# Block-sparse attention with an ELU feed-forward layer on one core: how K reaches the score matmuls, and who makes the chunk bounds

## The chip, the cores and the metric

The kernel runs on one core of a Trainium2 chip. The metric is the device time of one execution in microseconds (us). Three timed runs of the kernel before took 306.54, 306.47 and 304.36 us, median 306.47 us. The profile is one further execution of 304.14 us, whose instructions span 302.4 us.

## The reference

`q`, `k` and `v` are float32 of shape (4, 8, 768, 64): 4 batches, 8 heads, 768 positions, 64 features. Keys are cut into 24 chunks of 32 positions. For each query an upper bound on its scores in each chunk is made from the chunk's minimum and maximum key, the 6 best causal chunks are kept, and ordinary softmax attention runs over the kept keys. Two matrix products with ELU between them follow.

```python
k_chunks = k.reshape(B, H, nc, chunk, D)
k_min, k_max = np.min(k_chunks, axis=3), np.max(k_chunks, axis=3)
ub = np.sum(np.maximum(q[:, :, :, None, :] * k_min[:, :, None, :, :],
                       q[:, :, :, None, :] * k_max[:, :, None, :, :]), axis=-1)
ub = np.where(causal, ub, -1e9)
top_chunks = np.argsort(ub, axis=-1)[..., -6:]
scores = scale * np.matmul(q, k.transpose(0, 1, 3, 2))
scores = np.where(sel & causal_within, scores, -1e9)
x = softmax(scores) @ v                     # then (B*S, H*D) = (3072, 512)
h = x @ w_in                                # (3072, 2048)
g = np.where(h > 0.0, h, np.exp(np.minimum(h, 0.0)) - 1.0)
out = g @ w_out                             # (3072, 512)
```

## The kernel before

**Blocks and pairs.** The 3072 rows are nine query blocks (`BLOCKS`): batch 0 gives blocks 0 to 2 of 256 rows, batches 1 to 3 give blocks 3 to 8 of 384 rows, two each. Heads go in pairs, j = 0 to 3, so that a pair's 2 x 64 features fill 128 partitions. A tile is 128 positions.

**Front of a block** (`front`, lines 746 to 752). K, Q and V tiles are loaded as float32, 128 positions by 8 heads by 64 features, 256 KB each (`load`, L439). `prep_k` turns a pair's K tiles by TensorE into PSUM (`turn_in`, L480). VectorE reduces the turned K twice, maximum and minimum over each chunk of 32 columns (L500), and subtracts (L517); the results are the `ksts` operands of the bounds. ScalarE then copies the turned K to bfloat16: for blocks 0 and 1 straight into `lhs` (L507), for the others into a buffer `kb` (L512), from which SyncE's queue issues two transfers a pair into `lhs` (L515). `prep_q` does the same turning for Q (L480, L530, L538, L541). `select` multiplies the bounds on TensorE (L559), finds the sixth best chunk on VectorE (L570, L577, L581) and writes 0/1 rows into partitions 64 to 95 of `rhs`, either by VectorE (L587, blocks 0 to 2) or by VectorE and a transfer (L593, L597).

**Mask rows.** `lhs` has 96 used partitions: 64 features of K and 32 rows with -40000 in row c at the columns of chunk c. A score matmul over 96 rows (`scores`, L621) thus gives the score, plus -40000 where the chunk was not selected. The mask rows are made once (`make_eone`, `make_econst`, `init_lhs`): VectorE fills four of the eight `lhs` tensors (L415), four transfers fill the others (L417).

**Attention and feed-forward.** `attend`: scores (L621), exponent on ScalarE (L637, L641), the diagonal's triangle on VectorE (L648, L655), product with V (L670), division (L679, L681), turning to `xt` by a transposing transfer on SyncE's queue (L694) or by TensorE (L689). `mlp`: L709 on TensorE, exponent on ScalarE (L713), minus one on GpSimd (L715), `max`/`min` on VectorE to `gT` (L717), L728 on TensorE, copy out on ScalarE (L732), store (L735). V is cast to bfloat16 by GpSimd (`cast_v`, L471).

**Order.** Every operation is first only listed, with an assumed cost, a priority and its dependences. `Plan.run` then plays the list through, engine by engine, with limited buffers (`CAPS`) and a table of shifts of the priorities by stage and engine (`SHIFTS`); the order that comes out is the order in which the instructions are written to each engine, and each engine works through its own in that order. Loads named in `SW_LOADS` and the weights are issued by GpSimd in the order of `SW_ORDER`, after a small copy that waits for the first K load (L782). TensorE gets filler matmuls on a zero tile where the plan leaves it idle in its first 70 us (L836).

Of the kernel before, what the change touches and what calls it, by code (L numbers as in the profile page):

```python
# [48 lines left out]
DIRECT_K = (0,1)  # L49
# [4 lines left out]
SW_LOADS = ("v0", "q1", "v1", "k2", "q2", "v2")  # L54
ACT_LOADS = ("k0", "q0", "k1")
SW_ORDER = ("v0", "q1", "v1", "wi0", "wi1", "wi2", "wi3", "k2", "q2", "v2", "wo0", "wo1", "wo2", "wo3")
QC_ACT = (0, 1)
VC_ACT = ()
# [5 lines left out]
CAPS = dict(psT=1, psS=2, psO=1, psM=4, kld=2, qld=2, vld=1, QTf=6, Qrl=6, kb=3, kmx=3, ubT=2, thr=2,  # L64
            msk=2, pt=9, rcp=2, on=3, xt=12, gT=6, e=4, osb=2)
RING = 64
FILL_NS = 500
# [3 lines left out]
    ('cast', 'POOL'): (20.57252, 6.8612, 30.20405, 34.41781, 25.32335, 14.40461, 26.6349, 11.90162, 25.68724),  # L71
    ('gate', 'POOL'): (13.59135, 0.0, 0.0, 0.0, 0.0, 0.0, 0.0, 0.0, 0.0),
    ('init', 'POOL'): (0.0, 2.28733, 0.0, 0.0, 0.0, 0.0, 0.0, 0.0, 0.0),
    ('init', 'SP'): (0.0, 0.0, -9.16794, 0.0, 0.0, 0.0, 0.0, 0.0, 0.0),
    ('kld', 'ACT'): (8.44149, -3.35541, 0.0, 0.0, 0.0, 0.0, 0.0, 0.0, 0.0),
    ('kld', 'SP'): (2.64524, 1.41433, 0.0, 19.17193, 19.24991, 15.09263, 15.30211, 16.29283, 21.31107),
    ('kld', 'POOL'): (0.0, 0.0, 0.38774, 0.0, 0.0, 0.0, 0.0, 0.0, 0.0),
    ('mlp_in', 'ACT'): (-0.05814, -2.04884, 12.26157, -1.88135, -2.65088, -4.49011, 9.3327, 8.76113, -19.73093),
    ('mlp_in', 'DVE'): (-1.73242, 3.97867, -1.47336, 9.41966, -10.49042, -8.87396, -12.71275, -12.8411, -15.53763),
    ('mlp_in', 'PE'): (4.09513, -2.56825, 21.51914, 0.57236, -12.4212, 2.60542, -2.43752, -8.17452, 3.48831),  # L80
    ('mlp_in', 'POOL'): (-2.43649, 11.70673, 2.23367, -14.23721, -5.69178, 14.90153, -11.32679, 8.9361, -11.19179),
    ('mlp_out', 'ACT'): (-12.88274, 0.81443, 16.77095, 16.67571, -11.88345, 9.70583, 0.95732, -8.4172, -1.17404),
    ('mlp_out', 'PE'): (13.70296, 13.79101, 25.0585, 31.67234, 12.47262, 15.64879, 21.01371, 0.27209, 18.2925),
    ('mlp_out', 'SP'): (-3.30971, -11.51233, -15.89764, -18.24659, -18.60542, -17.81261, -26.35693, -42.75655, -13.10907),
    ('prep_k', 'ACT'): (25.42091, 28.44317, 23.77021, 23.42552, 13.97171, 21.34953, 15.42692, 18.62561, 8.78796),
    ('prep_k', 'DVE'): (-0.54594, 19.16199, -1.31495, -4.02643, 4.07559, 21.34444, 2.30963, 13.60589, 3.98678),
    ('prep_k', 'PE'): (-11.58195, 3.17776, 12.63442, -8.97337, 3.48395, 2.91992, -14.39538, 4.89175, 2.89372),
    ('prep_k', 'SP'): (0.0, 0.0, -5.13913, -2.5227, -2.19514, 2.12301, -17.34079, 2.83345, -3.2583),
    ('prep_q', 'ACT'): (-5.44132, 13.02836, -8.90449, 17.58325, 14.42173, 12.5627, 34.41294, 25.56545, -14.46432),
    ('prep_q', 'DVE'): (34.05268, 22.68609, 13.28254, 24.29798, 22.86233, 18.30023, 26.52607, 17.39426, -1.03575),  # L90
    ('prep_q', 'PE'): (1.55827, 3.21992, -10.06088, -5.14194, -2.06832, 11.30076, 4.84068, 13.28142, -17.29924),
    ('prep_q', 'POOL'): (0.0, 0.0, 5.34856, 19.77789, 11.98652, -3.89053, 10.37057, 11.76628, -23.71212),
    ('qld', 'ACT'): (3.03879, 0.0, 0.0, 0.0, 0.0, 0.0, 0.0, 0.0, 0.0),
    ('qld', 'SP'): (-1.86639, 0.0, 0.0, 4.4756, 10.84559, 7.56364, -2.78613, 8.55013, 3.96718),
    ('qld', 'POOL'): (0.0, -13.20166, -16.00657, 0.0, 0.0, 0.0, 0.0, 0.0, 0.0),
    ('score', 'ACT'): (10.38182, 13.98097, 9.11548, 19.0005, 2.98314, 27.9414, -1.05566, 1.31311, 14.18917),
    ('score', 'DVE'): (-19.79772, 4.15071, 2.99001, -22.45535, -14.99666, -19.5343, -10.56439, -19.58759, -3.51749),
    ('score', 'PE'): (-4.26638, 7.52896, -6.42214, -0.75335, 6.37057, 12.51955, 6.09242, -2.75776, -4.26028),
    ('select', 'DVE'): (0.47921, -15.73633, 7.03029, -0.12414, -12.38193, 6.31401, -10.30796, 14.19953, -5.33831),
    ('select', 'PE'): (-24.6966, -18.87682, -19.68284, -16.23997, -30.84817, 2.75471, -0.87585, -4.04933, -12.62166),  # L100
    ('select', 'SP'): (0.0, 0.0, 0.0, -13.44596, -16.7602, -5.46409, -14.4042, 14.89348, -7.20168),
    ('vld', 'POOL'): (8.78219, 3.38089, -2.61859, 0.0, 0.0, 0.0, 0.0, 0.0, 0.0),
    ('vld', 'SP'): (0.0, 0.0, 0.0, 33.2739, 30.57728, 28.35083, 33.49035, 19.69352, 14.95572),
    ('w_in', 'POOL'): (-4.9889, 0.0, 0.0, 0.0, 0.0, 0.0, 0.0, 0.0, 0.0),
    ('w_out', 'POOL'): (-8.71011, 0.0, 0.0, 0.0, 0.0, 0.0, 0.0, 0.0, 0.0),
    ('weigh', 'DVE'): (11.1506, -8.59523, 21.73165, 3.04344, -9.17916, -0.955, 14.23334, -3.50298, 13.22401),
    ('weigh', 'PE'): (-14.42242, 4.04006, -5.56916, -12.49286, -15.03128, -12.17144, 11.16201, -20.81204, -2.27982),
    ('weigh', 'SP'): (0.0, -24.05575, -20.27905, -10.4246, -14.45262, -3.75467, -21.17209, -15.72941, 0.0),
# [41 lines left out]
class Plan:  # L150
# [37 lines left out]
    def run(self):  # L188
# [41 lines left out]
        while True:  # L230
# [37 lines left out]
            if done is not None:  # L268
                done.end = clock + 750
                lanes[done.eng][done.lane] = done.end  # L270
                dirty.update(("SP", "ACT", "POOL"))
                leave(done, done.end)
                enter(done, done.end, True)
                continue
# [23 lines left out]
            else:  # L298
                o.end = t + o.occ + o.lat
# [7 lines left out]
def kernel(  # L307
# [37 lines left out]
    econst = fix([P, NCH, CHUNK], BF16, "econst")  # L345
    eone = fix([P, NCH], BF16, "eone")
# [3 lines left out]
    vexts = [fix([P, NQT, 2, D + 1], BF16, f"vext{s}") for s in range(NSET)]  # L350
    lhs = [fix([P, 2, S], BF16, f"lhs{s}") for s in range(NSET)]
    ksts = [fix([P, 2, NPAIR, CHUNK], F32, f"kst{x}") for x in range(2)]
    rhs = [fix([P, 2, NPAIR, w], BF16, f"rhs{x}") for x, w in enumerate((QMAX, QMAX, 256))]
# [4 lines left out]
    r_ident_f, r_ident_b, r_tri, r_econst, r_eone = res(), res(), res(), res(), res()  # L358
# [3 lines left out]
    r_lhs = [[res() for _ in range(3)] for _ in range(NSET)]  # L362
# [4 lines left out]
    RH = [{(0, 256): 0, (256, 512): 1, (512, 768): 2, (0, 384): 0, (384, 768): 1}[lo, hi] for (_b, _x, lo, hi) in BLOCKS]  # L367
# [25 lines left out]
    def make_eone():  # L393
        nc.gpsimd.memset(eone[64:96], MASKNEG)
        nc.gpsimd.affine_select(out=eone[64:96], in_=eone[64:96], compare_op=AOT.is_equal, fill=0.0, base=0,
                                pattern=[[1, NCH]], channel_multiplier=-1)

    pool_op(200, make_eone, [r_eone])
    pool_op(540, make_ident_f, [r_ident_f])

# [27 lines left out]
    def load(dst, x, i, cls, at):  # L428
# [5 lines left out]
        for n in range(nt):  # L434
# [9 lines left out]
            if e == "SP":  # L444
                chain[:] = [o]
# [422 lines left out]
```

## Time and profile before

| what | before |
|---|---|
| timed runs, median (lowest to highest) | 306.47 us (304.36 to 306.54) |
| the profiled execution, and its span | 304.14 us, 302.4 us |
| TensorE matmul busy | 279.0 us, 92% |
| VectorE, ScalarE, GpSimd busy | 204.9, 201.3, 138.9 us |
| mean granted TensorE clock | 0.960 |
| turning K on TensorE (L480) | 88 + 8 matmuls of 128 columns |
| VectorE reductions of K (L500) | 48 of 384 columns, 16 of 256 columns |
| ScalarE copies of K (L507, L512) | 16 and 28 |
| transfers from `kb` to `lhs` (L515) | 56, all issued by SyncE |

The page gives for each engine the time in which an instruction ran; matmuls overlap in the pipeline, so a busy TensorE is not one at its peak. The chain of waits follows the last instruction back to what released it. In a table by windows, the first column is the stretch of time, then its length, then busy time by engine with the number of instructions in parentheses, the granted clock, the mean busy share of the DMA engines, and GB/s. In a timeline, the columns are start, length, engine, line and operation; neighbouring instructions of one kind are merged with their number.

### The profile page before, as it was taken

What the parts mean: (1) busy time and instruction counts of PE and PEld (TensorE: products, weight loads), DVE (VectorE), ACT (ScalarE), POOL (GpSimd) and SP (SyncE); (2) the same over time, 40 slices, a digit from 0 to 9 for tenths busy, and PEclk for the clock granted to TensorE, in tenths of its full rate; (3) what the DMA queues carried; (4) which work ended last, traced back from release to release, by engine and by line L of the source; (5) the groups of instructions that cost most, each with busy time, mean ns of one, the idle gap of its engine ahead of it and who ended that gap; (6) DMA issues with size and microseconds to landing.
All of it is one profiled execution on the core that took longest, in us unless ns stands there. A gap on an engine that the chain in (4) does not pass through costs nothing.

```text
span 302.4 us, 7251 instructions
## 1 busy us (share of the span) xinstructions
PE 279.0 (92%) x2521; PEld 177.4 (59%) x2521; DVE 204.9 (68%) x658; ACT 201.3 (67%) x458; POOL 138.9 (46%) x285
## 2 busy tenths in 40 slices
PE   7466878999999899999999989999999999999994
PEld 7235645677857645666665546666556666554541
DVE  4567488799666979768579955874866646680420
ACT  1764767579829725997797259886398896671521
POOL 8796674024817624571069322581535100570420
PEclk9955797999999999999999999999999999999999
DMA  8769996149292565658239853924111012100101
GB/s 194 204 130 196 292 220 115 41 125 244 48 222 74 133 149 135 162 153 204 81 80 219 191 166 84 233 57 128 47 44 43 3 48 63 30 21 37 67 37 70
DMA packets 88805, 36.23 MB, mean 120 GB/s; under 512 B 76224, under 2 KB 84928, under 8 KB 88768
## 3 DMA queue, kind: packets, MB, share of 16 engines
q1 hardware_dynamic: 80464, 27.64, 36.3%
q0 software_dynamic: 5184, 7.34, 12.0%
q10 hardware_dynamic: 3120, 0.79, 1.2%
q8 instruction: 20, 0.33, 0.4%
q14 instruction: 17, 0.14, 0.1%
HBM read 27.26 MB, written 6.29 MB: 111 GB/s over the span
## 4 chain that ended last, share of the span: by engine, by line
PE 64%; DVE 14%; DMA 7%; POOL 6%; SPq 3%; ACT 2%; issue 2%; POOLq 0%; DVEq 0%; ACTq 0%
PE psM L728 22%; PE psM L709 18%; PE psS L621 10%; PE o_bank L670 6%; PE psT L480 5%; DVE gT L717 3%; DMA rhs<-msk 3%; DVE rhs L587 2%; POOL e L715 2%; SPq L439 2%; DMA vld<-in_v_dram 2%; DVE kmx L500 2%; PE psT L559 1%; DMA qld<-in_q_dram 1%; DVE pt L648 1%
## 5 line engine op out<-in xcount | busy, mean ns | idle before, releaser
L715 POOL TENSOR_SCALAR e<-e 128x384 f32<-128x384 f32 (+1 forms) x144 | 68.2, 479 | 106.4 <-ACT e L713 67.5
L709 PE MATMUL psM<-xt,w_in_sb 128*128 128x384 bf16 (+1 forms) x576 | 102.4, 313 | 1.8 <-DVE gT L717 1.5
L728 PE MATMUL psM<-w_out_sb,gT 128*128 128x512 bf16 x384 | 102.8, 379 | 0.0
L637 ACT ACTIVATE pt<-psS 128x384 bf16<-128x384 f32 (+1 forms) x164 | 83.4, 546 | 10.5 <-PE psS L621 9.0
L717 DVE SCALAR_TENSOR_TENSOR gT<-psM,e 128x384 bf16<-128x384 f32 (+1 forms) x144 | 70.8, 508 | 27.9 <-POOL e L715 24.6
L713 ACT ACTIVATE e<-psM 128x384 f32<-128x384 f32 (+1 forms) x144 | 66.0, 465 | 22.0 <-PE psM L709 20.5
L709 PEld LDWEIGHTS <-w_in_sb 128*128 128x128 bf16 x576 | 56.1, 100 | 29.5 <-issue 2.8
L621 PE MATMUL psS<-rhs,lhs 96*128 96x256 bf16 (+2 forms) x304 | 65.1, 287 | 4.3 <-DMA rhs<-msk 1.6
L728 PEld LDWEIGHTS <-gT 128*128 128x128 bf16 x384 | 36.3, 98 | 31.9 <-issue 2.1
L538 POOL TENSOR_SCALAR rhs<-QTf 64x384 bf16<-64x384 f32 (+1 forms) x56 | 29.7, 531 | 29.5 <-ACT QTf L530 21.9
L621 PEld LDWEIGHTS <-lhs 96*128 96x128 bf16 x312 | 28.2, 100 | 22.1 <-issue 4.3
L670 PEld LDWEIGHTS <-pt 128*128 128x128 bf16 x672 | 28.9, 99 | 11.2 <-DVE pt L648 2.1
L670 PE MATMUL o_bank<-vext,pt 128*128 128x65 bf16 x672 | 32.7, 195 | 2.0 <-DVE pt L648 1.3
L732 ACT ACTIVATE osb<-psM 128x512 f32<-128x512 f32 x24 | 14.5, 604 | 28.0 <-PE psM L728 27.9
L530 ACT ACTIVATE QTf<-psT 128x384 f32<-128x384 f32 (+1 forms) x32 | 15.3, 478 | 10.6 <-PE psT L480 10.2
L471 POOL TENSOR_SCALAR vext<-vld 128x384 bf16<-128x384 f32 (+1 forms) x36 | 17.4, 504 | 10.2 <-DMA vld<-in_v_dram 9.9
L648 DVE TENSOR_TENSOR pt<-pt,tri 128x512 bf16<-128x512 bf16 x36 | 17.1, 476 | 7.3 <-ACT pt L637 6.7
L512 ACT ACTIVATE kb<-psT 128x384 bf16<-128x384 f32 (+1 forms) x28 | 13.5, 483 | 11.8 <-DVE kst L500 8.0
L500 DVE TENSOR_REDUCE kmx<-psT 128x12 f32<-128x384 f32 (+1 forms) x32 | 16.5, 516 | 6.6 <-PE psT L480 6.3
L480 PE MATMUL psT<-ident_f,qld 128*128 128x128 f32 x88 | 16.5, 291 | 4.3 <-DMA qld<-in_q_dram 3.3
L541 DVE TENSOR_SCALAR Qrl<-QTf 128x192 f32<-128x192 f32 (+3 forms) x36 | 12.2, 349 | 10.3 <-ACT QTf L530 10.1
L681 DVE TENSOR_TENSOR on<-o_bank,rcp 128x384 bf16<-128x384 f32 (+1 forms) x36 | 18.3, 508 | 0.8 <-DVE rcp L679 0.3
(69 smaller groups left out, 241.7 us busy)
## 6 DMA issues: line engine op xcount, KB each, us to landing
out_dram<-osb SPq DMA_DIRECT2D x24, 256.0 KB, 2.2
kld<-in_k_dram SPq DMA_DIRECT2D x20, 256.0 KB, 3.7
qld<-in_q_dram SPq DMA_DIRECT2D x19, 256.0 KB, 4.2
vld<-in_v_dram SPq DMA_DIRECT2D x18, 256.0 KB, 3.7
lhs<-kb SPq DMA_DIRECT2D x48, 48.0 KB, 1.9
w_in_sb<-in_moe_w_in_dram POOLq DMA_DIRECT2D x4, 512.0 KB, 10.4
w_out_sb<-in_moe_w_out_dram POOLq DMA_DIRECT2D x4, 512.0 KB, 10.4
vld<-in_v_dram POOLq DMA_DIRECT2D x6, 256.0 KB, 4.3
```

The lines of the kernel that those rows point to most:

```text
L480: nc.tensor.transpose(ps.get()[:, P * n:P * (n + 1)], xb.get()[:, n, hs, :].rearrange("p h d -> p (h d)"), ident_f)
L500: nc.vector.tensor_reduce(out=out, in_=psk.get()[:, 0:w].rearrange("p (c w) -> p c w", w=CHUNK), axis=AX.X, op=o)
L538: pool_op(110 + pool_ns(w), lambda h=h: nc.gpsimd.tensor_scalar(out=rhs[RH[i]][0:64, h, j, 0:w], in0=qtf.get()[64 * h:64 * h + 64, 0:w], s ...
L621: nc.tensor.matmul(sps.get()[:, o + pc:o + pc + n], lhsT=lhs[s][0:96, hd, P * kb:P * (kb + 1)], rhs=rhs[y][0:96, hd, j, c0 - lo:c0 - lo + ...
L637: op("ACT", act_ns(wtot), 140, lambda pt=pt, sps=sps, hd=hd, wtot=wtot: nc.scalar.activation(out=pt.get()[:, hd, 0:wtot], in_=sps.get()[:, ...
L648: nc.vector.tensor_tensor(out=view, in0=view, in1=tri01[:, :].rearrange("p (a b w) -> p a b w", a=1, b=1) .to_broadcast([P, 2, 2, P]), op= ...
L670: nc.tensor.matmul(o3.get()[:, hd, qi, :], lhsT=pt.get()[:, hd, P * qt + off:P * qt + off + P], rhs=vexts[s][:, kb, hd, :], start=(kb == 0 ...
L709: op("PE", 1 + w / 2.4, 200, lambda fc=fc, kk=kk, h_ps=h_ps: nc.tensor.matmul(h_ps.get()[:, 0:w], lhsT=w_in_sb[:, kk, P * fc:P * (fc + 1)] ...
L713: op("ACT", act_ns(w), 200, lambda e=e, h_ps=h_ps: nc.scalar.activation(out=e.get()[:, 0:w], in_=h_ps.get()[:, 0:w], func=AF.Exp), reads=[ ...
L715: op("POOL", pool_ns(w), 72, lambda e=e: nc.gpsimd.tensor_scalar(out=e.get()[:, 0:w], in0=e.get()[:, 0:w], scalar1=-1.0, scalar2=1.0, op0= ...
L717: g_ops.append(op("DVE", dve_ns(w), 130, lambda e=e, h_ps=h_ps, fc=fc: nc.vector.scalar_tensor_tensor(out=gT[fc // 4].get()[:, fc % 4, 0:w ...
L728: op("PE", 216, 200, lambda tt=tt, fc=fc, o_ps=o_ps: nc.tensor.matmul(o_ps.get(), lhsT=gT[fc // 4].get()[:, fc % 4, P * tt:P * (tt + 1)], ...
```

## The change

For batches 1 to 3, TensorE no longer turns K, ScalarE no longer copies it, and VectorE no longer reduces it from PSUM. K goes two ways instead.

**K to `lhs`.** There are six fixed bfloat16 tensors `kns`, one per tile position: 128 positions by 8 heads by 128 columns. Columns 64 to 127 of each head are written once with the mask constants (`init_pads`, `init_kn`). Columns 0 to 63 get K: for batches 1 to 3 by a casting load that GpSimd issues (`load_kn`), for batch 0 by a GpSimd cast of the float32 tile (in `prep_k`). `turn_k` then issues, on SyncE's queue, one transposing transfer of 128 x 1024 elements a tile, which lands K and mask rows of all 8 heads in `lhs`. There are now two `lhs` tensors (batches alternate) in place of eight; `init_lhs` and its constants are gone.

**Bounds.** Batch 0 keeps its turning and reductions. For each later batch `bounds_k` loads K a second time, chunk-major: 96 partitions (4 heads x 24 chunks) by half a chunk (16 positions x 64 features, contiguous 4 KB), four loads a batch; VectorE reduces each twice over the 16 positions with a step of 64 elements between them; three small operations join the halves and subtract, TensorE turns the result by two small matmuls, and ScalarE copies it into `ksts` by four copies.

**With it.** V casts go by tile (512 elements) in place of by pair; Q and V buffers hold one tile each; memsets move from GpSimd to VectorE; `rhs` has two tensors in place of three; K of block 1 is loaded by GpSimd; the plan's assumed cost of a finished transfer rises from 750 to 1500 ns and 80 ns are added to each operation's latency; `SHIFTS` has other values.

```diff
-SW_LOADS = ("v0", "q1", "v1", "k2", "q2", "v2")
-ACT_LOADS = ("k0", "q0", "k1")
-SW_ORDER = ("v0", "q1", "v1", "wi0", "wi1", "wi2", "wi3", "k2", "q2", "v2", "wo0", "wo1", "wo2", "wo3")
+SW_LOADS = ("k1","q1","v0","v1","k2","q2","v2")
+ACT_LOADS = ("k0", "q0")
+SW_ORDER = ("k1","v0","q1","v1","wi0","wi1","wi2","wi3","k2","q2","v2","wo0","wo1","wo2","wo3")
-CAPS = dict(psT=1, psS=2, psO=1, psM=4, kld=2, qld=2, vld=1, QTf=6, Qrl=6, kb=3, kmx=3, ubT=2, thr=2,
+CAPS = dict(psT=1, psS=2, psO=1, psM=4, kld=3, qld=5, vld=3, QTf=5, Qrl=5, kmx=3, kpart=1, ubT=2, thr=2,
+DMA_END = 1500
+MARGIN = 80
...
+    def init_kn(t):
+        pool_op(600, lambda: nc.gpsimd.tensor_copy(
+            out=kns[t][:, :, D:P], in_=pads[:, t:t + 1, :].to_broadcast([P, H, D])), [r_kn[t]], [r_pads])
...
+    def load_kn(i):
+        b, _x, lo, hi = BLOCKS[i]
+        at = span(i - 2, 0.0, 1.0)
+        for t in range(lo // P, hi // P):
+            op("POOL", 890, (900, 159, 1000), lambda t=t: nc.gpsimd.dma_start(
+                out=kns[t][:, :, 0:D], in_=k[b, :, P * t:P * (t + 1)].rearrange("h p d -> p h d")), writes=[r_kn[t]])
+
+    def turn_k(i):
+        for t in range(lo // P, hi // P):
+            op("SP", 1400, (1000, 40, -100), lambda t=t: nc.sync.dma_start_transpose(
+                out=lhs[b % 2][:, :, P * t:P * (t + 1)], in_=kns[t][:, :, :].rearrange("p h r -> p (h r)")),
+                reads=[r_kn[t]], writes=[r_lhs[b % 2][t]])
+
+    def bounds_k(i):
+        at = span(i - 2, 0.0, 1.0)
+        part = buf("kpart", [P, 2, 2, 2, D], F32)
+        rows = 4 * NCH
+        for g in range(2):
+            for z in range(2):
+                ck = buf("kld", [P, CHUNK // 2 * D], F32)
+                o = op("SP", 600, dma(6, 4096), lambda g=g, z=z, ck=ck: nc.sync.dma_start(
+                    out=ck.get()[0:rows], in_=k[b, 4 * g:4 * g + 4].rearrange(
+                        "h (c z t) d -> z (h c) (t d)", z=2, t=CHUNK // 2)[z]), ...)
+                for w, how in enumerate((AOT.min, AOT.max)):
+                    op("DVE", 1140, 115, lambda g=g, z=z, ck=ck, w=w, how=how: nc.vector.tensor_reduce(
+                        out=part.get()[0:rows, z, g, w, :],
+                        in_=ck.get()[0:rows].rearrange("p (t d) -> p d t", d=D), axis=AX.X, op=how), ...)
+        op("DVE", 620, 120, diff, reads=[part], writes=[part])
+        op("PE", 200, 200, turn, reads=[part, r_ident_f], writes=[ps])
+        for w in range(2):
+            for h in range(2):
+                op("ACT", 150, 150, ...)          # into ksts, 64 partitions x 96
...
     def prep_k(j, i):
+        if j == 0:
+            for n in range(w // P):
+                op("POOL", pool_ns(512), 60, ...) # cast of the tile into kns
...
-        if i in DIRECT_K:
-            for h in range(2):
-                op("ACT", 60 + act_ns(w), 90, lambda h=h: nc.scalar.activation(
-                    out=lhs[s][0:64, h, lo:hi], in_=psk.get()[64 * h:64 * h + 64, 0:w], func=AF.Copy), ...)
-        else:
-            kb = buf("kb", [P, QMAX], BF16)
-            op("ACT", act_ns(w), 150, lambda: nc.scalar.activation(out=kb.get()[:, 0:w], ...))
-            for h in range(2):
-                op("SP", 590, dma(4, 2 * w), lambda h=h: nc.sync.dma_start(
-                    out=lhs[s][0:64, h, lo:hi], in_=kb.get()[64 * h:64 * h + 64, 0:w]), ...)
...
     def load_kq(i):
-        load(ldk, k, i, "kld", at)
+        if BLOCKS[i][0] == 0:
+            load(ldk, k, i, "kld", at)
+        else:
+            load_kn(i)
+            if BLOCKS[i][1] == 0:
+                bounds_k(i)
...
     def front(i):
-            prep_k(j, i)
+            if BLOCKS[i][0] == 0:
+                prep_k(j, i)
             prep_q(j, i)
+        turn_k(i)
         select(i)
```

## The prediction

> **What bounds the kernel now.** I read the span and the engines' shares first, then the slices of the granted clock, then the table by windows, then the chain of waits, and last the groups and single stretches that the change touches.
>
> ```profile
> span 302.4 us, 7251 instructions
> PE 279.0 (92%) x2521; PEld 177.4 (59%) x2521; DVE 204.9 (68%) x658; ACT 201.3 (67%) x458; POOL 138.9 (46%) x285
> ...
> PEclk9955797999999999999999999999999999999999
> ...
> PE 64%; DVE 14%; DMA 7%; POOL 6%; SPq 3%; ACT 2%; issue 2%; POOLq 0%; DVEq 0%; ACTq 0%
> ```
>
> TensorE (PE) is busy 92% of the span and holds 64% of the chain that ends last. The slices show two regimes: a start of about 50 us in which the clock drops to half and TensorE waits for loads and for short chains, and then a long stretch at full clock.
>
> ```profile
> 0.00:48.00 48.00, 32.80 (x300) 23.85 (x301) 30.78 (x113) 28.66 (x74) 38.02 (x83) 0.78 0.99 206
> 48.00:80.00 32.00, 31.60 (x349) 23.36 (x348) 28.07 (x96) 25.45 (x62) 9.84 (x23) 0.95 0.48 114
> 96.00:128.00 32.00, 30.27 (x259) 18.58 (x258) 27.91 (x89) 20.80 (x51) 16.53 (x35) 1.00 0.58 137
> 160.00:192.00 32.00, 30.36 (x240) 17.83 (x239) 23.48 (x71) 20.50 (x46) 14.07 (x29) 1.00 0.70 168
> 192.00:224.00 32.00, 31.86 (x322) 19.56 (x321) 23.88 (x95) 22.79 (x53) 15.99 (x31) 1.00 0.37 96
> ```
>
> Columns: window, length, PE, PE weight loads, DVE (VectorE), ACT (ScalarE), POOL (GpSimd), clock, DMA share, GB/s. From 48 us on TensorE has 0.1 to 1.7 us of idle time in 32, so work taken from it there shortens the kernel nearly one for one, if nobody else becomes late. VectorE is the next fullest: 28.07 and 27.91 us of 32 in two windows.
>
> **TensorE's part of the change.** The turning of K is costed by start to start, not by the pipelined length.
>
> ```profile
> 118.98 0.49 PE L480 MATMUL psT<-ident_f,kld 128*128 128x128 f32 x3
> 119.31 1.46 PE L709 MATMUL psM<-xt,w_in_sb 128*128 128x384 bf16 x8
> ```
>
> Three matmuls hold TensorE for 119.31 - 118.98 = 0.33 us. The kernel has 96 of them; batch 0 keeps 6 tiles x 4 pairs = 24, so 72 go, in 24 groups of three: 24 x 0.33 = 7.9 us. Added are two small turnings for each of three batches, at most 0.11 us each: 0.7 us. Sum: **-7.3 us**, all of it on the path.
>
> **ScalarE and VectorE.** These groups go or shrink:
>
> ```profile
> L500 DVE TENSOR_REDUCE kmx<-psT 128x12 f32<-128x384 f32 x24 | 13.1, 547 | 5.2 <-PE psT L480 5.0
> L500 DVE TENSOR_REDUCE kst<-psT 128x12 f32<-128x384 f32 x24 | 13.0, 543 | 0.0
> L512 ACT ACTIVATE kb<-psT 128x384 bf16<-128x384 f32 x24 | 12.0, 499 | 10.4 <-DVE kst L500 6.7 <-PE psM L709 3.3 <-DMA rhs<-msk 0.4
> L517 DVE TENSOR_TENSOR kst<-kmx,kst 128x12 f32<-128x12 f32 x24 | 4.9, 206 | 0.4
> L500 DVE TENSOR_REDUCE kmx<-psT 128x8 f32<-128x256 f32 x8 | 3.4, 421 | 1.4 <-PE psT L480 1.3
> L581 DVE TENSOR_TENSOR selb<-ubT,thr 128x288 bf16<-128x288 f32 x6 | 3.2, 573 | 0.0
> ```
>
> ScalarE loses 12.0 us here, 1.5 us of the 256-wide copies to `kb` and 5.9 us of the direct copies of blocks 0 and 1, and gains 12 copies of 96 elements, about 0.23 us each by the slope of the copies Q takes (509 ns at 384, 384 ns at 256): 2.7 us. That is -16.7 us, which I put at nothing: ScalarE's waits do not set the end.
>
> VectorE loses 13.1 + 13.0 + 4.9 = 31.0 us and gets 24 reductions of 1024 elements. The trace has no reduction with a step. The same instruction on neighbouring elements costs (547 - 421) / 128 = 0.98 ns an element, so 0.547 + 640 x 0.00098 = 1.18 us. The dearest row by element is the comparison L581, whose inputs are stepped and repeated: from 223 ns at 72 elements to 573 ns at 288 is 1.62 ns, or 0.573 + 736 x 0.00162 = 1.77 us. I take 1.18 us, the row of the same instruction and type, and keep 1.77 us as the far end. In total VectorE is then about even (24 x 1.18 = 28.3 us, plus three joins of about 0.8 us). But the work is moved: a batch's eight reductions now all stand before its first block's selection, where half of them stood before. In 48 to 80 us the table has 28.07 us, of which 4.4 + 0.9 us are block 3's reductions and subtractions; with 8 x 1.18 + 0.8 in their place it is 33.0, which is 1.0 us more than the window holds. By the same working 96 to 128 us gives 27.9 - 6.4 + 10.2 = 31.7 and 160 to 192 us gives 28.6, both inside. I count **+1.0 us**. The near end is -2 us (about what TensorE waits for VectorE after 48 us), the far end, at 1.77 us, is 5.7 + 4.5 + 1.3 = +11.5 us.
>
> A rule of the Trainium skill speaks against the change here. Its page "Vector Engine (DVE) Microarchitecture Reference", section "Measured stream behaviour on trn2 (trn3 not measured)", says that a port reads at full rate only in runs of two neighbouring words, and gives 1.73 ns a column for one source that hops at every element; the same section has a one-source case that hopped and stayed at full rate. By the hopping figure a reduction is an estimated 1024 x 1.73 + 75 ns = 1.85 us and the kernel would end near 311 us. No row of this trace has such a step, so the rule is not settled here.
>
> **GpSimd.** It gets 18 issues of `load_kn`, 0.93 us each by its 12 tile loads now (0.88 to 1.10 us): 16.7 us. With six `init_kn` and six casts of 512 elements at about 0.65 us (539 ns at 384, 433 ns at 256), two K loads of block 1 (1.9 us), less 5.8 us of memsets and 2 us saved by wider V casts, it comes to 139 + 19 = 158 us of 302. Behind each issue wait the minus-one steps L715 of the feed-forward chain.
>
> ```profile
> POOL e L715 <- ACT e L713: 67.5, 51, 11.1
> ```
>
> GpSimd itself waits 67.5 us for ScalarE in front of just those steps, and is idle 22, 15 and 18 us in the three windows above, where six issues (5.6 us) a batch fall. So **0**, with the idle time as cover; without it every issue would delay an L715 by up to 0.93 us. An issue also waits until `turn_k` has read the tile of the batch before, about one block earlier; if that were late, L715, then `gT`, then L728 would be.
>
> **SyncE and the transfers.** SyncE loses 56 issues at 0.6 us, four mask fills (4.0 us) and seven tile loads (4 us): 41 us; it gains 24 transposing issues. The 28 present ones take 1.21 us at the median, whether 256 or 384 columns wide; if the cost went by columns it would be 1.21 x 1024 / 384 = 3.2 us. I take 1.21: 29 us. So SyncE is freer by 12 us, or at the far end busier by 36 us, still with idle time left. Behind a `turn_k` that waits for its casting load stand stores and loads; the casting load is issued about two blocks ahead. A transposing transfer lands 2.4 us after its issue at 384 columns; 158 KB more at the 290 GB/s it reaches is 0.55 us more. K read twice adds 4.7 MB and the transposes about 6.3 MB to 36.2 MB, where the DMA share is 0.4 to 0.7. **0**; the price of a late tile is the 3.2 us that the mask transfer holds in the chain now.
>
> **The start.** TensorE waits 3.3 us for block 1's Q load, in front of block 0's selection:
>
> ```profile
> PE psT L480 <- DMA qld<-in_q_dram: 3.3, 2, 2.5
> ```
>
> GpSimd's memsets fill its queue to 8.77 us, and only then it issues V of block 0 and at 10.77 us this Q. After the change memsets are on VectorE, but two casts and two K loads (3.2 us) go ahead of that Q, from when K of block 0 has landed (first use at 7.31 us). The plan also assumes later landings (1500 for 750 ns), so the selection can go first. Ends: -3.3 us (the wait goes) and +3.2 us (Q and the weights come later). I take half of the wait, **-1.6 us**, since the fill of masks also leaves SyncE's queue.
>
> **Sum.** -7.3 + 1.0 + 0 + 0 - 1.6 = -7.9 us on 304.14 us, the profiled execution: 296.2 us. The median of the runs lies 306.47 - 304.14 = 2.3 us above that execution, so the forecast is **298.5 us**. A measurement here can tell about 1% (3 us) from no change. This case alone spans 293 to 303 us.
>
> **Rivals.** (1) *VectorE is the bound where the bounds are made* (slower). Place: VectorE's queue before the selections of blocks 3, 5 and 7, with `gT` behind it and L728 behind that. Price: at 1.77 us a reduction 11.5 us of overflow in place of 1.0, so 306.47 - 7.3 - 1.6 + 11.5 = 309.1 us, and 310.7 us if the start gives nothing. It decides from about 1.65 us a reduction, where the overflow equals the 8.9 us gained. For it: 28 of 32 us in two windows. Against: the same instruction at 0.98 ns an element. (2) *The gain is mostly given back on GpSimd*: 18 issues, of which a third meet a feed-forward run in which L715 is needed every 0.65 us, 6 x 0.93 = 5.6 us: 304 us. Against it speak the 67.5 us that GpSimd waits. (3) *The freed engines give more than TensorE's own work*: the start loses all 3.3 us and the 4 us that TensorE idles from 64 to 256 us go too: 306.47 - 7.3 - 3.3 - 4 = 292 us. For it: `psT` has one buffer, and K held it through a turning, two reductions and a copy, some 2 us a pair. (4) *The change does less than it says*: if K of batches 1 to 3 still passed TensorE there would be no gain, 306 us; the code leaves only batch 0 there, so I give it next to nothing.
>
> **How the numbers follow.** Forecast 0.50, rival 1 0.20, rival 2 0.17, rival 3 0.10, rival 4 and other causes 0.03. Faster by over 1% (below 303.4 us): nearly all of the forecast and rival 3, and a third of rival 2, 0.65. Slower by over 1% (above 309.5 us): rival 1, less its nearer part, plus strays, 0.20. Between: 0.15. The range 290 to 311 us leaves out about 0.08 at each side.
>
> **What would show it.** Right: 24 K turnings left on L480, TensorE's busy time down by about 11 us (its pipelined lengths), reductions near 1.2 us, TensorE idle under 2 us in the windows after 48 us, transposing issues near 1.2 us. Wrong: reductions of 1.7 us or more with TensorE waiting for `gT`; L715 waiting behind loads on GpSimd; score matmuls waiting for `lhs` landings; or a start in which the first feed-forward matmul comes later than its 30 us.

## The result and the profile after

The changed kernel is slower: 322.26 us at the median (320.66 to 324.66, four runs) against 305.54 us for the kernel before beside it. The ratio is 1.0555, with an interval of 1.0472 to 1.0638. The forecast was 298.5 us with a range of 290 to 311 us, so both the direction and the range were wrong. The profiled execution took 320.66 us. Ratios, and all medians below, leave out runs more than 1.5% above the fastest of the same kernel; `nochunk`, for which three expectations below give 304.2 us, thus stands at 303.3 us.

The head of the page and the shares of the chain that ended last:

```profile
span 319.0 us, 7007 instructions
PE 282.3 (89%) x2476; PEld 176.2 (55%) x2476; DVE 221.8 (70%) x630; ACT 190.0 (60%) x426; POOL 158.0 (50%) x294
...
PE   5767779389998779599987999999999999999995
...
PEclk9956999976999979979998799999999999999999
...
PE 54%; DVE 19%; DMA 10%; POOL 8%; ACT 3%; issue 3%; SPq 1%; DVEq 0%; ACTq 0%; POOLq 0%
```

TensorE has lost ten points of the chain (64% before). VectorE gained five and transfers three. The long stretch of full clock is broken: past the start, the slices of 6, 7 and 8 tenths lie in or right behind slices in which TensorE now waits (busy 3, 7, 5, 8 and 7 tenths). TensorE's busy time did not fall though work left it. Part of this is that the 576 feed-forward matmuls of L775 average 321 ns here, against 313 ns in the kernel before and 311 ns in `flat` below; the rest was not followed up.

The windows that the forecast looked at, and then two of 16 us; columns as before (PE, weight loads, DVE, ACT, POOL, clock, DMA share, GB/s):

```profile
48.00:80.00 32.00, 25.56 (x210) 16.08 (x208) 27.82 (x70) 16.06 (x37) 11.51 (x23) 0.84 1.59 185
96.00:128.00 32.00, 26.74 (x267) 17.89 (x266) 23.47 (x74) 22.17 (x50) 15.21 (x29) 0.95 0.92 140
160.00:192.00 32.00, 28.28 (x229) 16.07 (x214) 30.95 (x75) 18.18 (x39) 14.19 (x27) 0.89 0.72 133
```
```profile
48.00:64.00 16.00, 11.08 (x118) 7.05 (x116) 15.53 (x39) 4.44 (x12) 9.01 (x18) 0.99 1.79 169
128.00:144.00 16.00, 12.62 (x91) 7.48 (x90) 15.96 (x22) 7.30 (x17) 6.48 (x13) 0.89 1.06 162
```

TensorE's idle time in the three long windows grew from 0.4, 1.7 and 1.6 us to 6.4, 5.3 and 3.7 us. In both short ones VectorE is full (15.53 and 15.96 of 16 us); much of that is reductions for the bounds. The DMA share in 48 to 80 us went from 0.48 to 1.59, and that in a stretch where the forecast counted the transfers at nothing. In 96 to 128 us VectorE has room (23.47 of 32 us), yet TensorE idles too. Its longest wait there, 3.70 us to 113.67 us, is for a `gT` that has a transposing transfer (6.89 us from 104.38 us) and a casting load ahead of it in the chain: a second cause besides the reductions.

The new operations, from the page's groups and the list of DMA issues (last column: median us to landing):

```profile
L500 DVE TENSOR_REDUCE kpart<-kld 96x64 f32<-96x1024 f32 x24 | 44.6, 1887 | 0.0
L470 POOL DMA_DIRECT2D kn<-in_k_dram x18 | 16.4, 911 | 24.9 <-DMA lhs<-kn 23.8
```
```profile
kld<-in_k_dram SPq DMA_DIRECT2D x12, 384.0 KB, 5.6
...
kn<-in_k_dram POOLq DMA_DIRECT2D x18, 128.0 KB, 5.7
...
rhs<-msk SPq DMA_DIRECT2D x24, 24.0 KB, 2.0
xt<-on SPq DMA_TRANSPOSE x28, 2.8
lhs<-kn SPq DMA_TRANSPOSE x24, 4.5
rhs<-msk SPq DMA_DIRECT2D x24, 12.0 KB, 3.5
```

A stepped reduction takes 1.887 us. GpSimd stands 23.8 us in front of its casting loads, waiting for the transposing transfers of the batch before. The small 12 KB mask transfers, 1.8 us before, now take 3.5 us.

What the VectorE time does is seen in the chain near 125 us (start, length, what):

```profile
123.45 7.29 DVE kpart L500 x4
130.75 0.33 DVE pt L714
131.08 3.55 DVE kpart L500 x2
134.63 0.48 DVE gT L783
135.11 0.04 issue
135.15 0.86 PE psM L775 x3
```

Six reductions, 10.8 us, pass before VectorE gets to `gT`, and only then can TensorE multiply; it stood idle for 3.4 us. This is rival 1 at its place. The total, however, lies 13 us above the 309.1 us that rival gave, so the experiments had to find the rest.

### The profile page after: what moved, and what is told of

It reads as the page before. It is cut to its first block, busy times and chain, and to the rows that moved or that the text cites. A ratio compares the mean times of both kernels' runs of the same rounds, so it can differ in the third digit from the quotient of the medians.

```text
span 319.0 us, 7007 instructions
## 1 busy us (share of the span) xinstructions
PE 282.3 (89%) x2476; PEld 176.2 (55%) x2476; DVE 221.8 (70%) x630; ACT 190.0 (60%) x426; POOL 158.0 (50%) x294
## 4 chain that ended last, share of the span: by engine, by line
PE 54%; DVE 19%; DMA 10%; POOL 8%; ACT 3%; issue 3%; SPq 1%; DVEq 0%; ACTq 0%; POOLq 0%
PE psM L775 21%; PE psM L794 18%; DVE kpart L500 9%; PE psS L687 7%; DMA kld<-in_k_dram 5%; PE o_bank L736 4%; DMA vld<-in_v_dram 2%; DMA lhs<-kn 2%; DVE gT L783 2%; POOL e L781 2%; DVE pt L714 2%; PE psT L553 2%; ACT pt L703 1%; PE psT L625 1%; DMA rhs<-msk 1%
## 5 line engine op out<-in xcount | busy, mean ns | idle before, releaser
L781 POOL TENSOR_SCALAR e<-e 128x384 f32<-128x384 f32 (+1 forms) x144 | 69.5, 490 | 98.3 <-ACT e L779 76.9
L775 PE MATMUL psM<-xt,w_in_sb 128*128 128x384 bf16 (+1 forms) x576 | 108.4, 321 | 9.6 <-DVE gT L783 8.4
L775 PEld LDWEIGHTS <-w_in_sb 128*128 128x128 bf16 x576 | 57.3, 101 | 42.6 <-issue 15.3
L687 PE MATMUL psS<-rhs,lhs 96*128 96x384 bf16 (+2 forms) x304 | 65.0, 295 | 4.6 <-ACT pt L703 2.7
L500 DVE TENSOR_REDUCE kpart<-kld 96x64 f32<-96x1024 f32 x24 | 44.6, 1887 | 0.0
L687 PEld LDWEIGHTS <-lhs 96*128 96x128 bf16 x312 | 29.3, 103 | 25.9 <-issue 9.2
L736 PEld LDWEIGHTS <-pt 128*128 128x128 bf16 x672 | 29.1, 100 | 10.8 <-DVE pt L714 3.2
L470 POOL DMA_DIRECT2D kn<-in_k_dram x18 | 16.4, 911 | 24.9 <-DMA lhs<-kn 23.8
L919 PE MATMUL o_bank<-junk 128*128 128x112 bf16 x98 | 10.8, 274 | 11.5 <-DVE on L747 6.5
L542 POOL TENSOR_SCALAR vext<-vld 128x512 bf16<-128x512 f32 x24 | 15.3, 646 | 7.2 <-DMA vld<-in_v_dram 7.1
L607 DVE TENSOR_SCALAR Qrl<-QTf 128x192 f32<-128x192 f32 (+3 forms) x36 | 14.8, 426 | 5.2 <-ACT QTf L596 5.0
```

Of the source, the lines that this page charges most:

```text
L500: op("DVE", 1140, 115, lambda g=g, z=z, ck=ck, w=w, how=how: nc.vector.tensor_reduce(out=part.get()[0:rows, z, g, w, :], in_=ck.get()[0:ro ...
L687: nc.tensor.matmul(sps.get()[:, o + pc:o + pc + n], lhsT=lhs[b % 2][0:96, 2 * j + hd, P * kb:P * (kb + 1)], rhs=rhs[y][0:96, hd, j, c0 - l ...
L736: nc.tensor.matmul(o3.get()[:, hd, qi, :], lhsT=pt.get()[:, hd, P * qt + off:P * qt + off + P], rhs=vext[:, s, kb, hd, :], start=(kb == 0) ...
L775: op("PE", 1 + w / 2.4, 200, lambda fc=fc, kk=kk, h_ps=h_ps: nc.tensor.matmul(h_ps.get()[:, 0:w], lhsT=w_in_sb[:, kk, P * fc:P * (fc + 1)] ...
L781: op("POOL", pool_ns(w), 72, lambda e=e: nc.gpsimd.tensor_scalar(out=e.get()[:, 0:w], in0=e.get()[:, 0:w], scalar1=-1.0, scalar2=1.0, op0= ...
```

## The experiments

Times are medians; the ratio to the kernel before beside them stands with its interval. The kernel before stood at 303.2 to 305.3 us in these comparisons, so a difference between two runs of different comparisons is sure to some 2 us only.

**1. The price of the step.** Two kernels keep everything but the reading pattern of the 24 reductions. In `flat` each reads the same 1024 elements as neighbours (16 in a row for each result), in `thin` one row of 64. The bounds of batches 1 to 3 are then not the true ones.

```diff
-    in_=ck.get()[0:rows].rearrange("p (t d) -> p d t", d=D), axis=AX.X, op=how),
+    in_=ck.get()[0:rows].rearrange("p (d t) -> p d t", d=D), axis=AX.X, op=how),        # flat
+    in_=ck.get()[0:rows, 0:D].rearrange("p (t d) -> p d t", d=D), axis=AX.X, op=how),   # thin
```

Expected of `flat`: 

> The changed kernel with its 24 reductions of 1024 elements reading neighbouring elements in place of elements 64 apart; number, size and order of all instructions are the same (the bounds are those of wrong elements, so other chunks are selected). Theory A (the step between the elements makes a reduction dear, and VectorE's queue then holds up TensorE): a reduction falls from 1.89 to about 1.15 us, VectorE loses 18 us, and the time falls by 10 to 15 us to 307 to 312 us. Rival B (GpSimd's queue, which waits 23.8 us for transposing transfers in front of casting loads, sets the end): the time stays above 318 us.

Expected of `thin`: 

> The changed kernel with its 24 reductions reading 64 of the 1024 elements each; the rest of the reduction is left out, the order is the same. Theory A: a reduction costs about 0.15 us, VectorE loses 42 us, the time falls further than with neighbouring elements, to about 300 us, below the kernel before. Rival B: above 316 us.

Measured: `flat` 311.97 us, 1.0243 (1.0165 to 1.0322); `thin` 312.89 us, 1.027 (1.0183 to 1.0357). The group of `flat`, then that of `thin`:

```profile
L500 DVE TENSOR_REDUCE kpart<-kld 96x64 f32<-96x1024 f32 x24 | 28.2, 1203 | 6.2 <-DMA kld<-in_k_dram 6.2
```
```profile
L500 DVE TENSOR_REDUCE kpart<-kld 96x64 f32<-96x64 f32 x24 | 4.2, 202 | 6.2 <-DMA kld<-in_k_dram 6.2
```

The step alone is worth 322.26 - 311.97 = 10.3 us, for 44.6 - 28.2 = 16.4 us of VectorE. The other 24 us that `thin` takes away bring nothing, against the 300 us expected of it: with the chunk loads in place, the time of the reductions below 1.2 us each no longer sets the end. In both VectorE waits 6.2 us in front of them for the chunk loads' landing.

**2. The whole work without a step.** `fold` replaces each stepped reduction by minima or maxima of neighbouring columns, halving 512, 256, 128, 64 in place for one of a pair and in strips of 192 and 64 for the other.

```diff
-    op("DVE", 1140, 115, lambda ...: nc.vector.tensor_reduce(...))
+    op("DVE", 1140, 115, lambda ...: fold(g, z, ck, w, how))
+    # maximum:  for n in (512, 256, 128): x[0:n] = max(x[0:n], x[n:2n]);  part = max(x[0:64], x[64:128])
```

Expected of `fold`: 

> The changed kernel with the whole of its work: each stepped reduction of 1024 elements is replaced by a chain of minima or maxima of neighbouring elements, 4 operations of 512, 256, 128 and 64 columns in place for the second of a pair and 8 of 192 or 64 columns for the first. By the minimum and maximum rows at about 1 ns a column plus 0.06 us fixed these are an estimated 1.2 to 1.6 us in place of 1.89 us. If the step is what cost the 10 us, the run is at 312 to 316 us, and slower than the kernel before by 2 to 4%. If the plan's order or the place of the work is the cause, whatever its price, it stays at 320 us or more.

Measured: 324.0 us, 1.0603 (1.0519 to 1.0686). The estimate of its price was wrong:

```profile
L511 DVE TENSOR_TENSOR kld<-kld 96x512 f32<-96x512 f32 x12 | 9.2, 766 | 0.0
L511 DVE TENSOR_TENSOR kld<-kld 96x256 f32<-96x256 f32 x12 | 5.5, 459 | 0.4
```

Two float32 sources of 512 columns take 766 ns, not some 570. All its groups together are 48.4 us, 2.02 us for a reduction in place of 1.89, 3.8 us more of VectorE: the chain of halvings takes 1.79 us and the strips 2.25 us; the kernel is not told apart from the changed one (1.0555). So it is no mend, and as a test of "price or order" it says little by itself.

**3. The order, with the true price told to the plan.** `told1700` has all the work; the plan is given 1700 ns for 1140 ns and orders anew.

```diff
-    op("DVE", 1140, 115, lambda g=g, z=z, ck=ck, w=w, how=how: nc.vector.tensor_reduce(
+    op("DVE", 1700, 115, lambda g=g, z=z, ck=ck, w=w, how=how: nc.vector.tensor_reduce(
```

Expected of `told1700`: 

> The changed kernel with the plan's assumed cost of a reduction at 1700 in place of 1140 ns; nothing else is changed, but another order comes out. Theory A with a wrong order as its cause: the reductions are spread, TensorE's waits fall and the time goes to 310 to 316 us. Theory A with the price itself as cause: within 3 us of 322 us.

Measured: 324.42 us, 1.0666 (1.0567 to 1.0765). The order that came out with the same shifts did not hide the reductions; another table of shifts was not tried.

**4. Without the casting loads.** `nokn` leaves out the 18 casting loads of `load_kn`, so that `lhs` of batches 1 to 3 holds no K of theirs; `flat_nokn` does the same on `flat`.

```diff
-    op("POOL", 890, (900, 159, 1000), lambda t=t: nc.gpsimd.dma_start(out=kns[t][:, :, 0:D], ...), writes=[r_kn[t]])
+    op("POOL", 890, (900, 159, 1000), lambda: None, writes=[r_kn[t]])
```

Expected of `nokn`: 

> The changed kernel without the 18 casting loads of K that GpSimd issues: the transposing transfers of batches 1 to 3 move batch 0's K again, so these loads and what GpSimd waits for in front of them are left out. The order of all else is the same, the reductions still cost 1.89 us. Theory A: 316 to 321 us, since the reductions remain. Rival B: GpSimd's 23.8 us of waits go, and 8 us or more of the time with them, below 314 us.

Expected of `flat_nokn`: 

> Both earlier edits together: reductions over neighbouring elements (wrong elements, so other chunks are selected), and the 18 casting loads of K left out. If the price of the reductions (10 us) and GpSimd's casting loads with the waits in front of them (6 us) are separate causes, they add up: 305 to 307 us. If they hide each other, one of them alone is nearly all: 309 us or more.

Measured: `nokn` 316.39 us, 1.0403 (1.0327 to 1.048), 5.9 us under the changed kernel; `flat_nokn` 306.95 us, 1.0165 (1.005 to 1.028), 5.0 us under `flat`. The casting loads cost 5 to 6 us here, with or without the step.

**5. Without the chunk-major loads.** `nochunk` leaves out the 12 loads of K by chunks, and its reductions read a constant tile without a step (1.20 us each); `neither` leaves out the casting loads as well.

```diff
-    o = op("SP", 600, dma(6, 4096), lambda g=g, z=z, ck=ck: nc.sync.dma_start(out=ck.get()[0:rows], ...),
+    o = op("SP", 600, dma(6, 4096), lambda g=g, z=z, ck=ck: None,
...
+    in_=ident_f[0:rows, 0:D].rearrange("p (d t) -> p d t", t=1).to_broadcast([rows, D, CHUNK // 2]),
```

Expected of `nochunk`: 

> The changed kernel without its 12 chunk-major loads; the 24 reductions of 1024 elements read a constant tile with repeated elements in place of them (bounds of no use, so other chunks are selected), casting loads stay. Expected of the reductions alone (about 1.2 us each, as with neighbouring elements): 312 us. If the second reading of K and its late landing also hold up the bounds (10 us for one load at 58 us in the run with neighbouring elements): 305 to 309 us.

Expected of `neither`: 

> The changed kernel without chunk-major loads (reductions read a constant tile) and without the 18 casting loads; the order is the same. What is left is TensorE's 7.3 us less work and the new order. If stepping, casting loads and chunk loads are all of the loss: 296 to 300 us, the forecast. If the new order itself loses: 303 us or more.

Measured: `nochunk` 303.3 us, 1.0026 (0.9963 to 1.0088), 8.7 us under `flat`; `neither` 300.21 us, 0.9919 (0.9885 to 0.9953), 6.7 us under `flat_nokn` and 3.1 us under `nochunk`. The second reading of K was thus worth more than the casting loads. With both and the step gone, the kernel comes within 1.7 us of the forecast's figure, but it is only 3.0 us faster than the kernel before beside it (303.2 us), where the forecast had 8.0 us.

**6. Bytes or waits: the chunk loads.** `loose` issues the chunk loads in full but nobody reads them (reductions as in `nochunk`). `half` and `tiny` fetch 512 and 64 of the 1024 columns, with every issue and every wait of SyncE's queue for a buffer kept.

```diff
     # loose: the load as in the changed kernel, the reduction's in_ as in nochunk; in half and tiny also
-    out=ck.get()[0:rows], in_=k[b, 4 * g:4 * g + 4].rearrange("h (c z t) d -> z (h c) (t d)", ...)[z]),
+    out=ck.get()[0:rows, 0:64], in_=k[b, 4 * g:4 * g + 4].rearrange("h (c z t) d -> z (h c) (t d)", ...)[z, :, 0:64]),
```

Expected of `loose`: 

> The changed kernel in which the twelve chunk-major loads are still issued, but the 24 reductions read a constant tile (contiguous, repeated) and so do not wait for them: the bounds of batches 1 to 3 are not computed from K. Flat reads with the loads took 312.0 us, the same without the loads 304.2 us. If those 7.7 us are VectorE standing in its queue until a chunk load has landed, this run is near 304 to 306 us and TensorE's waits for gT shrink as they did without the loads. If they are the transfers themselves (4.7 MB more, beside the casting loads and the tile loads, and the issues on SyncE), it stays near 311 to 312 us. The transfers' issues, 12 x 384 KB, stay in both cases.

Expected of `half`: 

> The same with 512 of the 1024 columns in each chunk load (192 KB). If the price goes by bytes it is about halfway between the run without chunk loads and the one with full ones, 307 to 309 us. If it is the held queue, 310 to 313 us, as with 64 columns.

Expected of `tiny`: 

> As the run in which the reductions read a constant tile while the chunk-major loads are still issued, but each of the twelve chunk loads fetches 64 of its 1024 columns (24 KB in place of 384 KB). Its issues, their place in SyncE's queue and their waits for a kld buffer stay as they were; only the bytes go. With the full loads it took 312.5 us, with no loads 304.2 us. If the price is the bytes (4.7 MB beside the other transfers), this run is at 304 to 306 us. If it is SyncE's queue, held for 15 us where a chunk load waits for a buffer, it stays at 310 to 313 us.

Measured: `loose` 312.45 us, 1.0241 (1.0192 to 1.029); `half` 306.6 us, 1.0042 (1.0003 to 1.008); `tiny` 305.3 us, 0.9993 (0.9953 to 1.0033). Nobody waiting for the data changed nothing (312.45 against 311.97 us of `flat`); taking the bytes away took 7.1 us. SyncE's queue is held as long without the bytes: in `tiny` it waits 8.7 us for the buffer of one chunk load, in `loose` 9.0 us, and its longest wait but for stores, at L761, is 16.3 us against 15.8 us. So the queue's wait for a buffer is not the cause; what is left of it in `tiny`, with its issues and 24 KB a load, is 2.0 us over `nochunk`. Half the bytes cost 3.3 us over `nochunk`, all of them 9.1 us. In proportion to the bytes between `tiny` and `loose`, `half` would be at 308.6 us; it is 2.0 us lower, which is no more than two comparisons can differ, so whether the price is in proportion stays open.

Three pieces of the chain of `loose`:

```profile
102.55 6.04 DMA lhs<-kn
...
109.12 0.73 POOL kn L470
...
110.06 0.43 POOL e L782
110.49 0.02 issue
110.52 0.43 DVE gT L784
...
155.90 2.43 DMA rhs<-msk
...
164.00 7.04 DMA qld<-in_q_dram
```

In the first, a transposing transfer takes 6.04 us, the casting load that will overwrite its source waits for it on GpSimd, the minus-one step (L782 here) stands behind that load, and `gT` behind the step. It is not in the chain of `nochunk`, but it stands in that of `tiny` as well, where the transposing transfer takes 6.48 us from 100.84 us. So it is not what the bytes of the chunk loads add. The two traces, 7.2 us apart, show where that falls. Their feed-forward matmuls come in the same order; the 161st starts at 110.99 us in `loose` and at 109.72 us in `tiny`, the 241st at 140.11 and 139.24 us, the 257th at 163.25 and 159.45 us, the 289th at 176.64 and 169.23 us. Nearly all is lost between 140 and 177 us.

The other two pieces lie there. TensorE waits 2.55 us for the mask transfer that is issued at 155.90 us, and 2.1 us in two waits for Q tiles, one of which lands 7.04 us after its issue. In `tiny` it has neither wait in this stretch. VectorE has written the mask at 151.5 us, but the transfer stands in SyncE's queue behind two transposing transfers, whose issue takes twice as long as in `tiny`, where the mask is written at 150.3 us and its transfer issued at once (the timelines of SyncE's queue, `loose` and then `tiny`; columns: start, length):

```profile
148.98 5.53 SPq L477 DMA_TRANSPOSE lhs<-kn  x2
```
```profile
146.32 2.62 SPq L477 DMA_TRANSPOSE lhs<-kn  x2
```

The bytes thus act through the landings of others and through the issues in SyncE's queue. This is read from one execution of each kernel. The two waits are 4.6 us of the 6.5 us lost there; what lengthened the two issues is not shown.

**7. Bytes or issues: the casting loads.** `kntiny` is `nochunk` with casting loads of one head of eight.

```diff
-    out=kns[t][:, :, 0:D], in_=k[b, :, P * t:P * (t + 1)].rearrange("h p d -> p h d"))
+    out=kns[t][:, 0:1, 0:D], in_=k[b, 0:1, P * t:P * (t + 1)].rearrange("h p d -> p h d"))
```

Expected of `kntiny`: 

> The run without chunk-major loads (304.2 us), in which each of the 18 casting loads fetches one head of eight (16 KB written in place of 128 KB): the issues on GpSimd and their waits for the transposing transfers stay, seven eighths of the bytes go. Without any casting loads it took 300.2 us. If the 4.0 us between them are the bytes, this run is near 300 to 301 us; if they are GpSimd's issues and their waits, it is near 303 to 305 us.

Measured: 301.15 us, 0.9879 (0.9847 to 0.991): 2.2 us of the 3.1 us between `nochunk` and `neither` are gone, and by the ratios (`neither` 0.9919) all of them.

```profile
L470 POOL DMA_DIRECT2D kn<-in_k_dram x18 | 10.2, 566 | 18.4 <-DMA lhs<-kn 17.8
```

GpSimd still waits 17.8 us in front of these loads (19.0 in `nochunk`), and each issue takes 566 ns in place of 907 ns. So the waits by themselves cost next to nothing. What costs is the bytes, or the longer issues that go with them: 6 us of issue time in sum went away too, and the two can't be told apart here. The landings moved too: the 12 KB mask transfers take 2.0 us at the median in place of 3.3, the 256 KB Q loads 4.1 in place of 4.6.

**8. What TensorE's part is worth.** `twice` is the kernel before with each K turning of batches 1 to 3 done twice.

```diff
-            for n in range(nt):
+            for n in [*range(nt)] * (2 if two else 1):
...
-        turn_in(psk, k_ld, w // P)
+        turn_in(psk, k_ld, w // P, b > 0)
```

Expected of `twice`: 

> The kernel before with every turning of K of batches 1 to 3 on TensorE done twice, 72 matmuls more, the order is the same. If 0.11 us a matmul comes off one for one when they are taken away, as the forecast counted, adding them costs 7.9 us: 312 to 315 us. If they stand in time that TensorE waits anyway: below 309 us.

Measured: 310.85 us, 1.0267 (1.0122 to 1.0413), or 8.1 us, between 3.7 and 12.6. The forecast's 7.9 us for 72 turnings lies inside, in a wide interval; and it is the price of added turnings in the old order, not the gain of removed ones in the new.

**9. Half the change, without shifts.** `before0` is the kernel before with all entries of `SHIFTS` at zero. `psum0` has K go to `lhs` in the new way, but keeps TensorE's turning and VectorE's reductions from PSUM for the bounds of all batches, also at zero shifts.

```diff
-    ('cast', 'POOL'): (20.57252, 6.8612, 30.20405, ...),     # every row, in both kernels
+    ('cast', 'POOL'): (0.0, 0.0, 0.0, ...),
...
-        if BLOCKS[i][0] == 0:                                # psum0: float32 K tiles for every block,
-            load(ldk, k, i, "kld", at)                       # two kld buffers of three tiles
-        else:
+        load(ldk, k, i, "kld", at)
+        if BLOCKS[i][0] > 0:
             load_kn(i)
-            if BLOCKS[i][1] == 0:
-                bounds_k(i)
...
-            if BLOCKS[i][0] == 0:
-                prep_k(j, i)
+            prep_k(j, i)
```

Expected of `before0`: 

> The kernel before with all hand-tuned time shifts of its order set to zero, so that the plan alone orders the work. It serves as the base for the next run, whose order has no shifts either. Slower than the kernel before by 2 to 6%: 312 to 325 us. The shifts are a search's result for one set of operations; if they are worth more than 5%, part of the changed kernel's loss could sit in its shifts rather than in its operations.

Expected of `psum0`: 

> Only the first half of the change, with no time shifts: K reaches lhs by casting loads and transposing transfers, but the bounds of all batches are still made by TensorE turning K and by VectorE reducing the turned tile; no chunk-major loads, no stepped reductions. Against the unshifted kernel before: ScalarE loses its copies to lhs, SyncE its mask fills, GpSimd gains 18 casting loads and K is read twice. If the casting loads and their waits cost 4 to 6 us by themselves, it is 0 to 6 us above the unshifted kernel before; if freeing psT of the copies and SyncE of the mask fills is worth more than they cost, it is 2 to 6 us below.

Measured: `before0` 321.6 us, 1.0542 (1.0455 to 1.0628); `psum0` 323.84 us, 1.0614 (1.0551 to 1.0677). The two are not told apart. The first half of the change gives nothing in an unshifted order: what it frees on ScalarE and SyncE pays for the casting loads at most. And the table of shifts is worth some 5% to the kernel before, about as much as the changed kernel lost. Whether a better table would give the changed kernel part of it back stays open; the changed kernel with no shifts was not tried.

No kernel with the whole work was faster than the kernel before.

## Why the prediction was wrong

**Where 23.8 us went.** The forecast was 298.5 us, the kernel takes 322.3. The runs give a ladder: 10.3 us for the step (to `flat`), 8.7 us for the chunk loads (to `nochunk`), 3.1 us for the casting loads (to `neither`). That is 22.1 us, and `neither`, at 300.2 us, lies 1.7 us above the forecast. The steps are not quite independent: the casting loads are worth 5.9 us on the changed kernel and 3.1 us at the ladder's foot, the step 9.4 us where the casting loads are left out (`nokn` to `flat_nokn`).

All of this loss falls between 48 and 184 us. The starts of the feed-forward matmuls put the changed kernel 0.6 us behind `neither` at 48 us, 5.4 us at 75 us, 21.0 us at 184 us and 21.1 us at the end.

That `neither` ends so near the forecast is partly luck. The forecast set out from 306.47 us, and the kernel before stood at 303.2 us beside `neither`: of the 8.0 us of gain some 5 us did not come even without the three costs. In 48 to 80 us TensorE of `neither` is busy for 27.92 of 32 us, against 31.60 before. Which term that belongs to stays open.

**The step that failed first: VectorE's +1.0 us.** The working was right and the duration in it was not. It took the row of the same instruction, 0.98 ns an element on neighbours, for a reading with a step of 64 elements, and set aside the row with a stepped source, L581 at 1.62 ns. (That figure comes from two of the row's widths; the other two, 501 ns at 128 elements and 348 ns at 192, do not lie on its line.) Measured: 1.887 us, 1.84 ns an element, and 1.203 us for the same elements as neighbours (the forecast's 1.18). The far end, 1.77 us, had been the nearer row, because the pattern of the reading was what set the price (1.887 against 1.203 us for the same operation). The difference between the two ends, 11.5 - 1.0 = 10.5 us, is close to the 10.3 us of the experiment, but partly by chance: the same working at the measured 1.887 and 1.203 us gives 14.3 - 1.2 = 13.1 us. Rival 1 came true at its place (`gT` behind the reductions) and with about its price, but it is less than half of what the forecast missed; the chance of 0.20 was too low for it.

By the Trainium skill, page "Vector Engine (DVE) Microarchitecture Reference", section "Measured stream behaviour on trn2 (trn3 not measured)", 1.73 ns a column for one source that hops 4 KiB at every element made an estimated 1.85 us. The trace, with 256 bytes from one element to the next, comes close to it with 1.887 us.

**The step that failed second: "SyncE and the transfers: 0".** It was given no price but that of a late tile, on the ground of a DMA share of 0.4 to 0.7. The transposing issues take 1.32 us at the median (1.21 counted), as was judged, and the queue's waits for a buffer cost 2.0 us at most. But 4.7 MB of chunk loads and 18 casting loads fall into the stretch of 22 to 190 us, where the share rises to 1.59, and transfers that TensorE depends on are issued and land later. `loose` against `tiny` is 7.1 us of bytes alone, `nochunk` against `kntiny` 2.2 us of bytes and shorter issues. In `loose` nobody waits for the chunk loads, and yet they cost this, by way of others' transfers. Which ones is shown for two places of one trace, the mask transfer and the Q tile of experiment 6.

**GpSimd: 0.** Its busy time came out as counted, 158.0 us. The wait for `turn_k` that the forecast named is real (23.8 us), and it stands in the chain of the changed kernel, but `kntiny` keeps 17.8 us of it and ends 0.9 us from `neither`. The term was not 0 all the same: the casting loads cost 3.1 to 5.9 us, which takes in rival 2's 5.6 us. Whether its reason, the issues ahead of the minus-one steps, or the bytes are behind that is not shown.

**TensorE: -7.3 us.** 24 K turnings are left, as counted, and `twice` puts 72 at 8.1 us (3.7 to 12.6). Its busy time rose by 3.3 us instead of falling by 11, in part because the feed-forward matmuls of L775 show longer (321 against 313 ns, at a mean granted clock of 0.941 against 0.960); even in `neither` it is 273.9 us, 5 us less than before. That sign was a poor one to watch.

**The start: -1.6 us.** Not tested by itself. The first feed-forward matmul starts at 30.0 us, against 30.1 us before, so up to there nothing was gained or lost. What follows comes in another order than before, and whether any of the 1.6 us came stays open.

**The signs named beforehand.** Of those for "wrong", two came: reductions of 1.7 us or more with TensorE waiting for `gT` (8.4 us by the waits), and the minus-one step (L715 before) waiting behind loads on GpSimd. The second cost little by itself.

## What to carry to other kernels

Price a new operand by the row whose access pattern it shares, before the row that shares its operation: moved to an engine that is full where it falls, most of the difference is paid (here 10.3 of 16.4 us). Count added transfers at the place where they run, not by the mean share, and ask whose transfers they delay; here loads that nobody waited for cost 7 us, about as much as the turnings they were to replace. A kernel whose order was tuned for one set of operations can lose some 5% by its order alone, as the kernel before did without its shifts, so an edit's own worth is best read from runs that share an order.

## What the runs showed of the hardware

- The same float32 reduction of 96 x 1024 elements takes 1.203 us on neighbours and 1.887 us with 64 elements between them; a maximum of two float32 sources of 512 contiguous columns takes 0.766 us, so a chain of such halvings down to 64 columns (1.79 us) is hardly cheaper than the stepped reduction.
- A transposing transfer of 128 x 1024 bfloat16 elements holds its issuer hardly longer at the median than one of 256 or 384 columns did (1.32 against 1.21 us), though two of them held it 5.53 us beside full chunk loads and 2.62 us beside small ones; it lands after 3.4 us at the median with few other loads (`neither`), 4.5 us in the changed kernel and 4.9 us in `loose`.
- Twelve loads of 384 KB that nobody read made the kernel 7.1 us slower than twelve of 24 KB in the same places, and 5.8 us slower than twelve of 192 KB.
- The issue of a casting load on GpSimd is longer for a larger load: 0.91 us for 128 KB, 0.57 us for 16 KB.
